# Attention block and MLP on one core: projection weights read in place, in pairs, instead of through a permuted copy

## The chip, the cores and the metric

The kernel runs on one core of a Trainium2 chip. The metric is the device time in microseconds of one execution. Profiled times come from one further execution, recorded by the hardware profiler: its span runs from the first to the last instruction, and its own time is somewhat longer than the span.

## The reference

One sequence of 2048 rows, 576 columns, bf16. `A_*` and `B_*` are the inputs.

```python
def _A_ref(x, wqkv, wo):          # x: layer norm of the input
    H = 32; Dh = 18; W, dil = 8, 2
    qkv = (x @ wqkv).reshape(B, S, 3, H, Dh).transpose(2, 0, 3, 1, 4)
    q, k, v = qkv[0], qkv[1], qkv[2]
    idx = pos[:, None] - arange(W)[None, :] * dil      # 8 keys: the row itself, 2 back, 4 back ...
    kg, vg = k, v gathered at idx                      # (B, H, S, W, Dh)
    logits = einsum("bhsd,bhswd->bhsw", q, kg) * Dh ** -0.5   # idx < 0 masked with -1e9
    attn = softmax(logits)
    o = einsum("bhsw,bhswd->bhsd", attn, vg)
    return o.transpose(0, 2, 1, 3).reshape(B, S, D) @ wo

def _B_ref(x, w1, b1, w2, b2):    # hidden width 4608
    return gelu(layernorm(x) @ w1 + b1) @ w2 + b2

h = x + _A_ref(layernorm(x), wqkv, wo)
out = h + _B_ref(h, w1, b1, w2, b2)
```

A column of the Q, K or V part of `wqkv` is numbered by head and dimension: column `h * 18 + d`.

## The kernel before

The 2048 rows are dealt to 16 tiles of 128 rows so that row `16 p + j` lies in partition `p` of tile `j`. The key that lies two rows back is then in the same partition, in the tile two before, and the eight keys of a row are eight tiles of one parity. `kwin[e]` and `vwin[e]` hold the eight K and V tiles of parity `e`. When tile `n` has been used, its K and V slots are replaced by the same tile shifted by one partition, through DRAM (`kvd`, written by `bounce`, read back into the slots by the loads `ks` and `vs`, lines 520 and 522). Row 0 of `kvd` is zero.

The work is written as named tasks with an engine, a cost, a priority and the tasks that must come first. `Weaver.run` is a planner: it takes, again and again, the ready task that could start first by the costs, and issues its instructions. Each engine then runs its instructions in that order; the costs decide the order and nothing else. Buffers are counted as slots in the planner (`pm`, three PSUM tiles; `lg`, `prod`, `q` and so on).

The tasks of a tile `n`:

- `ln1a`, `ln1r`, `ln1b`: layer norm. VectorE takes the statistics (line 314), their aggregate (315) and the variance with the epsilon (`ln_var`, 318), GpSimd raises it to the power -1/2 (322), VectorE (tiles 0 to 7) or ScalarE (357, tiles 8 to 15, with `nmr` from GpSimd, 349) normalizes in place.
- `t1`, `t1e`: the transposition, for tiles 0 to 7 by TensorE (329) and a copy by ScalarE (373), for the others by a DMA. The transposed tiles 0 to 6 lie for a while in the space of `vwin[1]`, those of later tiles in `kwin[1]`, which gives the names in the profile.
- `cK`, `cV`, `cQ`: the projections (394), a chunk each of two halves of 288 columns times five blocks of 128 rows of the contraction, so ten matmuls with a moving operand `wqkv_sb` of 128 x 288. `eK`, `eV`, `eQ`: eviction to bf16 by ScalarE (406).
- `p1a` to `p1b`, `ex`, `p2n`, `p2a`, `p2s`, `p2b`: the attention, on VectorE but for the exponential (ScalarE, 468). K times q for eight slots at once (445, 4608 elements); a tree of additions over the 18 dimensions (451) and the last addition into `lg` (458); maximum over the slots (438 to 440), difference (464); after the exponential the sum over the slots (again 438 to 440), its reciprocal (476) and `at = lg * rden` (479); V times `at` (486) and a tree over the slots (492 to 498).
- `t2`, `wo`, `woe`, `ln2a`, `hb`, `ln2m`, `ln2b`, `t3`: output projection (564), residual (577), second layer norm and its transposition.

Two tiles form a group `g` of the MLP: nine units `u` (630: first matrix; 641: gelu on ScalarE), then the second matrix in four passes (667), and the addition of `hb` on VectorE (686) and the store.

The tree of line 451 needs all heads of one dimension side by side, that is columns numbered `d * 32 + h`. The kernel gets this order by permuting the weights: the Q, K and V parts of `wqkv` are loaded into `wraw`, and 15 copies, `perm{t}{kt}` (line 290, six on ScalarE, nine on VectorE), write them to `wqkv_sb` in the other order, reading every 18th element. The K copies come first; those of V and Q are put on ScalarE and VectorE between the tasks of tiles 2 to 8. `wo` is loaded with its rows in the same order (`wo_load`, 212). `wraw` and `zrow`, the zero row for `kvd`, lie in a pool that is closed before the first part of `w2` is loaded, into the same space (`w2_chunk`, 236); that load waits for all permutations.

SP issues nearly all DMAs in the planned order: x tiles, V and Q weights, biases, `wo`, `w1` (18 parts, 223), the transposes (371, 541), the bounces (426, 427), `w2` (18 parts). ScalarE's queue issues the K weights.

Of the kernel before, what the change touches and what calls it, by code (L numbers as in the profile page):

```python
# [90 lines left out]
def kernel(  # L91
# [48 lines left out]
    wo_sb = wpool.tile([P, KC, HALF], BF16, name="wo_sb")  # L140
    hn_bufs = [wpool.tile([P, KC, 2 * P], BF16, name="hnT0")]
    b1_raw = wpool.tile([FT, P], BF16, name="b1_raw")
# [13 lines left out]
    raw_cm = tc.tile_pool(name="raw", bufs=1, side="right")  # L156
    raw = raw_cm.__enter__()
    wraw = raw.tile([P, 3, KT, D], BF16, name="wraw")
    zrow = raw.tile([NT, 2 * D], BF16, name="zrow")

    late, w2p = {}, {}
# [35 lines left out]
    def wq_load(eng, t, k0, k1):  # L197
        def fn():
            src = bass.AP(tensor=A_wqkv.tensor, offset=A_wqkv[k0 * P, t * D].offset,
                          ap=[[3 * D, P], [P * 3 * D, k1 - k0], [1, D]])  # L200
            eng.dma_start(out=wraw[:, t, k0:k1, :], in_=src)
        return fn

    def wq_rest(eng, t):
        return lambda: eng.dma_start(out=wraw[0:64, t, 4, :], in_=A_wqkv[512:576, t * D:(t + 1) * D])

    def wo_load(half, dd):
        def fn():
            src = bass.AP(tensor=A_wo.tensor, offset=A_wo[dd, half * HALF].offset,
                          ap=[[Dh * D, H], [2 * D, KC], [1, HALF]])  # L210
            p0 = 64 * half + 32 * dd
            nc.sync.dma_start(out=wo_sb[p0:p0 + 32, :, :], in_=src)
        return fn
# [12 lines left out]
    def b1_load():  # L226
        nc.sync.dma_start(out=b1_raw[:], in_=B_b1.rearrange("(f p) -> f p", p=P))

    def w2_chunk(c):
        def fn():  # L230
            if "w2" not in w2p:
                raw_cm.__exit__(None, None, None)
                pool = ctx.enter_context(tc.tile_pool(name="w2p", bufs=1, side="right"))
                w2p["w2"] = pool.tile([P, FT, D], BF16, name="w2_sb")
            f0, f1 = c * FT // W2C, (c + 1) * FT // W2C
            nc.sync.dma_start(out=w2p["w2"][:, f0:f1, :],
                              in_=B_w2[f0 * P:f1 * P, :].rearrange("(ft p) c -> p ft c", p=P))
        return fn
# [16 lines left out]
    def b2_load():  # L255
        nc.sync.dma_start(out=b2_bc[:], in_=B_b2.partition_broadcast(P))
        nc.sync.dma_start(out=kvd[:, 0, :], in_=zrow[:])
# [3 lines left out]
    wos = [f"WO{half}{dd}" for half in range(2) for dd in range(2)]  # L261
    for half in range(2):
        for dd in range(2):
            bulk(f"WO{half}{dd}", wo_load(half, dd), 166, prio=10)
# [5 lines left out]
    perms = [f"perm{t}{kt}" for t in range(3) for kt in range(KT)]  # L270
    for c in range(W2C):
        bulk(f"w2{c}", w2_chunk(c), 295, prio=30 + c, after=perms + ["b2"])
# [7 lines left out]
    nc.gpsimd.memset(zrow[:], 0.0)  # L280
# [3 lines left out]
    for t in range(3):  # L284
        for kt in range(KT):
            def perm(t=t, kt=kt, on=None):
                rows = P if kt < KT - 1 else D - kt * P
                src = wraw[0:rows, t, kt, :].rearrange("p (h d) -> p d h", h=H, d=Dh)
                dst = wqkv_sb[0:rows, kt, t * D:(t + 1) * D].rearrange("p (d h) -> p d h", d=Dh, h=H)
                {"ACT": nc.scalar.copy, "DVE": nc.vector.tensor_copy}[on](out=dst, in_=src)  # L290
            on = "ACT" if kt in (1, 3) else "DVE"
            add(f"perm{t}{kt}", on, {"ACT": 1.23, "DVE": 0.65}[on], lambda f=perm, on=on: f(on=on),
                (f"W{t}{'aabbc'[kt]}",) + ((("ln1b0",) if kt == 2 else ()) if t == K else (f"t1e{2 + 2 * t}" if on == "ACT" else f"ln1b{W - 1}",)),
                prio=(-18, -100, -17)[t])
# [43 lines left out]
    def front(n):  # L338
# [36 lines left out]
        add(f"ln1a{n}", "DVE", 1.2, ln1a, (f"x{n}",) + (("ln1b0",) if n == 1 else ()), prio=-20 + n if n < W else 0.5 + (n - W) // 4)  # L375
        add(f"ln1r{n}", "POOL", 0.6 if n < W else 1.1, ln1r, (f"ln1a{n}",), prio=-20, lag=0.1 if n < W else 1.0)
# [10 lines left out]
        def chunk(t):  # L387
            def fn():
                pq = ps_pm.tile([P, 2, 512], F32, tag="pm", name="pq")
                T["pq", n, t] = pq  # L390
                for half in range(2):
                    c0 = t * D + half * HALF
                    for kt in range(KT):
                        nc.tensor.matmul(pq[:, half, 0:HALF], lhsT=T["xnT", n][:, kt, :],  # L394
                                         rhs=wqkv_sb[:, kt, c0:c0 + HALF],
                                         start=(kt == 0), stop=(kt == KT - 1))
            return fn

        def evict(t):
            def fn():  # L400
                if t == Q:
                    T["q", n] = wpool.tile([P, D], BF16, tag="q", name="q", bufs=NQ)
                    dst = T["q", n][:]
                else:
                    dst = (kwin if t == K else vwin)[e][:, s, :]
                nc.scalar.copy(out=dst.rearrange("p (a c) -> p a c", a=2), in_=T["pq", n, t][:, :, 0:HALF])  # L406
            return fn
# [23 lines left out]
    def attention(n):  # L431
# [16 lines left out]
        def p1b(steps):  # L448
            pv = T["prod", n][:].rearrange("p w (d h) -> p w d h", d=Dh, h=H)
            for a, b in steps:  # L450
                nc.vector.tensor_tensor(out=pv[:, :, 0:b - a, :], in0=pv[:, :, 0:b - a, :],  # L451
                                        in1=pv[:, :, a:b, :], op=ALU.add)
# [17 lines left out]
        def p2n():  # L470
# [6 lines left out]
            at = sb.tile([P, W, H], BF16, tag="at", name="at", bufs=1)  # L477
            T["at", n] = at
            nc.vector.tensor_tensor(out=at[:], in0=lg[:], in1=rden[:].unsqueeze(1).to_broadcast([P, W, H]),
                                    op=ALU.mult)  # L480

        def p2a():
# [22 lines left out]
        add(f"p1s{n}", "DVE", 1.37, lambda: p1b(((9, 18),)), (f"p1a{n}",), prio=n)  # L505
        add(f"p1t{n}", "DVE", 1.5, lambda: p1b(((4, 8), (2, 4), (1, 2))), (f"p1s{n}",), prio=n)
# [6 lines left out]
        add(f"p2n{n}", "DVE", 1.35, p2n, [f"ex{n}"] + ([f"p2a{n - 1}"] if n else []), prio=-8 + n, give=(f"lg{n}",))  # L513
# [103 lines left out]
    def mlp(g):  # L617
# [115 lines left out]
```

## Time and profile before

| | |
|---|---|
| median of 3 runs | 390.32 us (389.94 to 390.32) |
| the profiled execution | 389.9 us, of it span 388.1 us |
| TensorE's granted clock over the span | 1.000 |
| TensorE, matmuls | 373.1 us busy, 4607 instructions |
| VectorE | 297.1 us, 559 |
| ScalarE | 220.5 us, 447 |
| GpSimd | 37.2 us, 65 |
| projections (394), matmuls | 480, in 210 + 210 + 60 by the tile that holds the transposed rows |
| share of the 16 DMA engines, 6.7 to 26.5 us | 1.0 |

Times are in microseconds from the start of the span unless marked ns. PE is TensorE, PEld its weight loads, DVE VectorE, ACT ScalarE, POOL GpSimd, SP the engine that issues DMAs. A group line names the source line, engine, operation, output from input, shapes and count; then busy time and the mean duration of one in ns; then the idle time of the engine just before and what ended it. Matmuls are pipelined: the mean duration of one is longer than its share of a row of them, which the timeline shows. A line of the waits reads: who waited, for whom, us in total, how often, the longest.

### The profile page before, as it was taken

What the parts mean: (1) busy time and instruction counts of PE and PEld (TensorE: products, weight loads), DVE (VectorE), ACT (ScalarE), POOL (GpSimd) and SP (SyncE); (2) the same over time, 40 slices, a digit from 0 to 9 for tenths busy, and PEclk for the clock granted to TensorE, in tenths of its full rate; (3) what the DMA queues carried; (4) which work ended last, traced back from release to release, by engine and by line L of the source; (5) the groups of instructions that cost most, each with busy time, mean ns of one, the idle gap of its engine ahead of it and who ended that gap; (6) DMA issues with size and microseconds to landing.
All of it is one profiled execution on the core that took longest, in us unless ns stands there. A gap on an engine that the chain in (4) does not pass through costs nothing.

```text
span 388.1 us, 10761 instructions
## 1 busy us (share of the span) xinstructions
PE 373.1 (96%) x4607; PEld 305.2 (79%) x4607; DVE 297.1 (77%) x559; ACT 220.5 (57%) x447; POOL 37.2 (10%) x65
## 2 busy tenths in 40 slices
PE   2889999999899999999999999999999999999996
PEld 1667877788777887887788878887888788778875
DVE  5999999999999999999999998989976952000000
ACT  4697767688914974188227823790487068306700
POOL 6455010101001000001100010110011011000000
PEclk9999999999999999999999999999999999999999
DMA  8988899887232402127333214222312432100000
GB/s 264 277 165 227 213 212 272 254 255 235 57 83 51 105 19 61 33 63 63 70 77 73 61 48 94 63 47 76 78 37 43 108 64 21 29 15 19 2 15 17
DMA packets 63968, 38.48 MB, mean 99 GB/s; under 512 B 39520, under 2 KB 63904, under 8 KB 63920
## 3 DMA queue, kind: packets, MB, share of 16 engines
q1 hardware_dynamic: 63296, 37.13, 40.4%
q8 instruction: 36, 0.59, 0.7%
q10 hardware_dynamic: 624, 0.66, 0.5%
q14 instruction: 12, 0.10, 0.1%
HBM read 22.28 MB, written 6.52 MB: 74 GB/s over the span
## 4 chain that ended last, share of the span: by engine, by line
PE 74%; DVE 12%; issue 1%; ACT 1%; DVEq 0%; ACTq 0%
PE po L667 37%; PE pm L630 33%; PE pw L564 4%; DVE prod L445 3%; DVE prod L451 2%; DVE prod L486 1%; ACT hT L641 1%; DVE prod L492 1%; DVE l_st L314 1%; DVE h L577 1%; DVE hb L590 1%; DVE half L438 0%; DVE prod L496 0%; DVE half L439 0%; DVE lg L458 0%
## 5 line engine op out<-in xcount | busy, mean ns | idle before, releaser
L641 ACT ACTIVATE hT<-pm,b_sb 128x256 bf16<-128x256 f32 x288 | 111.9, 482 | 82.1 <-PE pm L630 81.8
L630 PE MATMUL pm<-hnT,w_sb 64*128 64x256 bf16 x2592 | 144.5, 269 | 0.8 <-ACT hT L641 0.8
L667 PE MATMUL po<-w_sb,hT 128*128 128x288 bf16 x1152 | 143.2, 286 | 0.0
L630 PEld LDWEIGHTS <-w_sb 64*128 64x128 bf16 x2592 | 125.9, 94 | 17.7 <-issue 2.4
L667 PEld LDWEIGHTS <-hT 128*128 128x128 bf16 x1152 | 111.7, 98 | 30.6 <-issue 2.4
L686 DVE TENSOR_TENSOR osb<-po,hb 128x288 bf16<-128x288 f32 x32 | 14.4, 453 | 57.1 <-PE po L667 57.1
L322 POOL TENSOR_TENSOR l_rs<-l_ve,mhalf 128x1 f32<-128x1 f32 x32 | 28.4, 888 | 287.8 <-DVE l_ve L318 287.8
L451 DVE TENSOR_TENSOR prod<-prod 128x2304 bf16<-128x2304 bf16 (+1 forms) x64 | 44.2, 690 | 1.8
L486 DVE TENSOR_TENSOR prod<-vwin,at 128x4608 bf16<-128x4608 bf16 x16 | 40.9, 2554 | 0.4
L445 DVE TENSOR_TENSOR prod<-kwin,q 128x4608 bf16<-128x4608 bf16 x16 | 40.9, 2555 | 0.3
L394 PE MATMUL pq<-wqkv_sb,vwin 128*128 128x288 bf16 x210 | 30.1, 303 | 3.2 <-ACT vwin L373 1.8
L594 ACT ACTIVATE hn<-h,nmr,l_rs 128x576 bf16<-128x576 f32 (+1 forms) x32 | 19.2, 651 | 23.0 <-issue 11.6
L394 PEld LDWEIGHTS <-vwin 128*128 128x128 bf16 x210 | 21.2, 103 | 10.5 <-ACT vwin L373 2.6
L394 PE MATMUL pq<-wqkv_sb,kwin 128*128 128x288 bf16 x210 | 27.2, 286 | 0.0
L394 PEld LDWEIGHTS <-kwin 128*128 128x128 bf16 x210 | 20.3, 98 | 5.4 <-issue 0.5
L492 DVE TENSOR_TENSOR prod<-prod 128x2304 bf16<-128x2304 bf16 x16 | 21.7, 1358 | 0.6
L569 ACT COPY h<-pw 128x576 f32<-128x576 f32 x16 | 10.4, 651 | 19.4 <-PE pw L564 19.4
L564 PE MATMUL pw<-wo_sb,oT 64*128 64x288 bf16 x288 | 20.3, 283 | 0.0
L577 DVE TENSOR_TENSOR h<-h,xr 128x576 f32<-128x576 f32 x16 | 12.0, 752 | 9.6 <-ACT h L569 9.6
L564 PEld LDWEIGHTS <-oT 64*128 64x128 bf16 x288 | 13.5, 94 | 4.5 <-issue 1.4
L406 ACT CAST kwin<-pq 128x576 bf16<-128x576 f32 x16 | 10.2, 648 | 8.5 <-PE pq L394 8.3
L314 DVE BATCH_NORM_STATS2 l_st<-h 128x6 f32<-128x288 f32 x32 | 13.1, 452 | 0.6
(62 smaller groups left out, 238.2 us busy)
## 6 DMA issues: line engine op xcount, KB each, us to landing
w_sb<-in_B_w_dram SPq DMA_DIRECT2D x36, 288.0 KB, 4.7
xr<-in_A_x_dram SPq DMA_DIRECT2D x16, 144.0 KB, 2.3
out_dram<-osb SPq DMA_DIRECT2D x16, 144.0 KB, 1.8
kvd<-kwin SPq DMA_DIRECT2D x14, 144.0 KB, 4.1
kvd<-vwin SPq DMA_DIRECT2D x14, 144.0 KB, 3.7
kwin<-kvd SPq DMA_DIRECT2D x14, 144.0 KB, 2.5
vwin<-kvd SPq DMA_DIRECT2D x14, 144.0 KB, 2.1
wraw<-in_A_wqkv_dram SPq DMA_DIRECT2D x4, 288.0 KB, 4.1
```

The costliest lines, as they stand in the source:

```text
L314: nc.vector.bn_stats(out=st[:, c, :], in_=src[:, c * HALF:(c + 1) * HALF])
L322: nc.gpsimd.tensor_tensor(out=L["rs"][:, n, :], in0=L["ve"][:, n, :], in1=mhalf[:], op=ALU.pow)
L394: nc.tensor.matmul(pq[:, half, 0:HALF], lhsT=T["xnT", n][:, kt, :], rhs=wqkv_sb[:, kt, c0:c0 + HALF], start=(kt == 0), stop=(kt == KT - 1))
L445: nc.vector.tensor_tensor(out=prod[:], in0=kwin[e][:], in1=T["q", n][:].unsqueeze(1).to_broadcast([P, W, D]), op=ALU.mult)
L451: nc.vector.tensor_tensor(out=pv[:, :, 0:b - a, :], in0=pv[:, :, 0:b - a, :], in1=pv[:, :, a:b, :], op=ALU.add)
L486: nc.vector.tensor_tensor(out=prod[:].rearrange("p w (d h) -> p w d h", d=Dh, h=H), in0=vwin[e][:].rearrange("p w (d h) -> p w d h", d=Dh, ...
L492: nc.vector.tensor_tensor(out=prod[:, 0:4, :], in0=prod[:, 0:4, :], in1=prod[:, 4:8, :], op=ALU.add)
L564: nc.tensor.matmul(pw[:, half, 0:HALF], lhsT=T["oT", n][lo:lo + 64, block(c, half), :], rhs=wo_sb[lo:lo + 64, c, :], start=(c == 0), stop= ...
L594: nc.scalar.activation(out=hn_slots[n % 2][:, c0:c1], in_=src, func=ACT.Identity, scale=L2["rs"][:, n, :], bias=nmr[:, n, :])
L630: nc.tensor.matmul(pm[:, half, q, 0:width], lhsT=w1_sb[lo:lo + 64, c, f0:f0 + P], rhs=T["hnT", g][lo:lo + 64, block(c, half), 0:width], st ...
L641: nc.scalar.activation(out=T["hT", g, u][:, half, q, 0:width], in_=T["pm", g, u][:, half, q, 0:width], func=ACT.Gelu_apprx_tanh, bias=b1_s ...
L667: nc.tensor.matmul(T["po", n, half][:], lhsT=T["hT", g, u][:, r, q, a * P:(a + 1) * P], rhs=w2p["w2"][:, ft, half * HALF:(half + 1) * HALF ...
```

## The change

The permutation is gone. The weights are loaded into `wqkv_sb` as they are, and the matmul's moving operand is a strided view of them: for a half, nine pairs of dimensions `k`, 16 heads `h` and the two dimensions `r` of a pair, two adjacent elements and then a step of 18 elements (36 bytes). The projection comes out as `k, h, r` within a half, and the eviction puts the two halves together to `k, (h, r)`, rows of 64. The tree over the dimensions becomes one over the nine pairs, the last addition is over `r`, and `at` is written twice, for both `r`, so that V times `at` has rows of 64. `wo`'s rows are loaded to match, to every second partition.

With it, `w2_sb` gets space of its own from the start; `b1_raw` and the zero row lie in it until its parts are loaded. For tiles 0 to 7 `ln_var` goes from VectorE to GpSimd. Four costs in the planner are changed (`ln1a`, `ln1r`, `p2n`, and the `perm` tasks are gone), so the planner's order moves in places: of the first tiles, the second and third transposes of TensorE follow each other, and the first Q chunk comes before the eighth K chunk; in SP's queue some `w1` parts come later, and eight instead of five parts of `w2` follow a K reload.

```diff
+    w2_sb = wpool.tile([P, FT, D], BF16, name="w2_sb")
+    b1_raw = w2_sb[0:FT, 2, 0:P]
...
-    wraw = raw.tile([P, 3, KT, D], BF16, name="wraw")
-    zrow = raw.tile([NT, 2 * D], BF16, name="zrow")
...
-            eng.dma_start(out=wraw[:, t, k0:k1, :], in_=src)
+            eng.dma_start(out=wqkv_sb[:, k0:k1, t * D:(t + 1) * D], in_=src)
...
-            p0 = 64 * half + 32 * dd
-            nc.sync.dma_start(out=wo_sb[p0:p0 + 32, :, :], in_=src)
+            nc.sync.dma_start(out=wo_sb[64 * half + r:64 * half + 64:2, :, :], in_=src)
...
-        nc.sync.dma_start(out=kvd[:, 0, :], in_=zrow[:])
+        nc.sync.dma_start(out=kvd[:, 0, :], in_=w2_sb[0:NT, 0:2, :].rearrange("p a c -> p (a c)"))
...
-        bulk(f"w2{c}", w2_chunk(c), 295, prio=30 + c, after=perms + ["b2"])
+        bulk(f"w2{c}", w2_chunk(c), 295, prio=30 + c, after=("b2", "b1t"))
...
-    for t in range(3):
-        for kt in range(KT):
-            def perm(t=t, kt=kt, on=None):
-                rows = P if kt < KT - 1 else D - kt * P
-                src = wraw[0:rows, t, kt, :].rearrange("p (h d) -> p d h", h=H, d=Dh)
-                dst = wqkv_sb[0:rows, kt, t * D:(t + 1) * D].rearrange("p (d h) -> p d h", d=Dh, h=H)
-                {"ACT": nc.scalar.copy, "DVE": nc.vector.tensor_copy}[on](out=dst, in_=src)
...
         def ln1a():
             ln_stats(L1, n, T["x", n][:, 0:D])
-            ln_var(nc.vector, L1, n, (1.0, EPS))
+            if n >= W:
+                ln_var(nc.vector, L1, n, (1.0, EPS))
 
         def ln1r():
+            if n < W:
+                ln_var(nc.gpsimd, L1, n, (1.0, EPS))
             ln_rstd(L1, n)
...
-                    c0 = t * D + half * HALF
                     for kt in range(KT):
+                        cols = wqkv_sb[:, kt, t * D:(t + 1) * D].rearrange("p (h k r) -> p k h r", h=H, r=2)
                         nc.tensor.matmul(pq[:, half, 0:HALF], lhsT=T["xnT", n][:, kt, :],
-                                         rhs=wqkv_sb[:, kt, c0:c0 + HALF],
+                                         rhs=cols[:, :, half * H // 2:(half + 1) * H // 2, :],
                                          start=(kt == 0), stop=(kt == KT - 1))
...
-                nc.scalar.copy(out=dst.rearrange("p (a c) -> p a c", a=2), in_=T["pq", n, t][:, :, 0:HALF])
+                nc.scalar.copy(out=dst.rearrange("p (k a c) -> p a k c", a=2, c=H),
+                               in_=T["pq", n, t][:, :, 0:HALF].rearrange("p a (k c) -> p a k c", c=H))
...
-            pv = T["prod", n][:].rearrange("p w (d h) -> p w d h", d=Dh, h=H)
+            pv = T["prod", n][:].rearrange("p w (k c) -> p w k c", c=2 * H)
...
-            nc.vector.tensor_tensor(out=lg[:], in0=pv[:, :, 0, :], in1=pv[:, :, 8, :], op=ALU.add)
+            nc.vector.tensor_tensor(out=lg[:], in0=pv[:, :, :, 0], in1=pv[:, :, :, 1], op=ALU.add)
...
-            at = sb.tile([P, W, H], BF16, tag="at", name="at", bufs=1)
+            at = sb.tile([P, W, H, 2], BF16, tag="at", name="at", bufs=1)
...
-            nc.vector.tensor_tensor(out=at[:], in0=lg[:], in1=rden[:].unsqueeze(1).to_broadcast([P, W, H]),
-                                    op=ALU.mult)
+            nc.vector.tensor_tensor(out=at[:], in0=lg[:].unsqueeze(3).to_broadcast([P, W, H, 2]),
+                                    in1=rden[:].unsqueeze(1).unsqueeze(3).to_broadcast([P, W, H, 2]), op=ALU.mult)
...
-                                    in1=at[:].unsqueeze(2).to_broadcast([P, W, Dh, H]), op=ALU.mult)
+            pairs = at[:].rearrange("p w h r -> p w (h r)")
+                                    in1=pairs.unsqueeze(2).to_broadcast([P, W, Dh // 2, 2 * H]), op=ALU.mult)
...
-        add(f"p1s{n}", "DVE", 1.37, lambda: p1b(((9, 18),)), (f"p1a{n}",), prio=n)
-        add(f"p1t{n}", "DVE", 1.5, lambda: p1b(((4, 8), (2, 4), (1, 2))), (f"p1s{n}",), prio=n)
+        add(f"p1s{n}", "DVE", 1.37, lambda: p1b(((5, 9),)), (f"p1a{n}",), prio=n)
+        add(f"p1t{n}", "DVE", 1.5, lambda: p1b(((3, 5), (2, 3), (1, 2))), (f"p1s{n}",), prio=n)
```

More of the change, by code (lines that the diff above doesn't have):

```diff
@@ L140 @@
     wo_sb = wpool.tile([P, KC, HALF], BF16, name="wo_sb")
+    w2_sb = wpool.tile([P, FT, D], BF16, name="w2_sb")
+    b1_raw = w2_sb[0:FT, 2, 0:P]
     hn_bufs = [wpool.tile([P, KC, 2 * P], BF16, name="hnT0")]
-    b1_raw = wpool.tile([FT, P], BF16, name="b1_raw")
     b1_sb = wpool.tile([P, FT], F32, name="b1_sb")
@@ L155 @@
     wqkv_sb = early.tile([P, KT, 3 * D], BF16, name="wqkv_sb")
-    raw_cm = tc.tile_pool(name="raw", bufs=1, side="right")
-    raw = raw_cm.__enter__()
-    wraw = raw.tile([P, 3, KT, D], BF16, name="wraw")
-    zrow = raw.tile([NT, 2 * D], BF16, name="zrow")
-    late, w2p = {}, {}
+    late = {}
     def late_pool():
@@ L200, in fn, with wo_load @@
                           ap=[[3 * D, P], [P * 3 * D, k1 - k0], [1, D]])
-            eng.dma_start(out=wraw[:, t, k0:k1, :], in_=src)
+            eng.dma_start(out=wqkv_sb[:, k0:k1, t * D:(t + 1) * D], in_=src)
         return fn
     def wq_rest(eng, t):
-        return lambda: eng.dma_start(out=wraw[0:64, t, 4, :], in_=A_wqkv[512:576, t * D:(t + 1) * D])
-    def wo_load(half, dd):
+        return lambda: eng.dma_start(out=wqkv_sb[0:64, 4, t * D:(t + 1) * D], in_=A_wqkv[512:576, t * D:(t + 1) * D])
+    def wo_load(half, r):
         def fn():
-            src = bass.AP(tensor=A_wo.tensor, offset=A_wo[dd, half * HALF].offset,
+            src = bass.AP(tensor=A_wo.tensor, offset=A_wo[r, half * HALF].offset,
                           ap=[[Dh * D, H], [2 * D, KC], [1, HALF]])
-            p0 = 64 * half + 32 * dd
-            nc.sync.dma_start(out=wo_sb[p0:p0 + 32, :, :], in_=src)
+            nc.sync.dma_start(out=wo_sb[64 * half + r:64 * half + 64:2, :, :], in_=src)
         return fn
@@ L226, in b1_load @@
     def b1_load():
-        nc.sync.dma_start(out=b1_raw[:], in_=B_b1.rearrange("(f p) -> f p", p=P))
+        nc.sync.dma_start(out=b1_raw, in_=B_b1.rearrange("(f p) -> f p", p=P))
     def w2_chunk(c):
         def fn():
[L231 to L234, printed above, removed]
             f0, f1 = c * FT // W2C, (c + 1) * FT // W2C
-            nc.sync.dma_start(out=w2p["w2"][:, f0:f1, :],
+            nc.sync.dma_start(out=w2_sb[:, f0:f1, :],
                               in_=B_w2[f0 * P:f1 * P, :].rearrange("(ft p) c -> p ft c", p=P))
@@ L256, in b2_load @@
         nc.sync.dma_start(out=b2_bc[:], in_=B_b2.partition_broadcast(P))
-        nc.sync.dma_start(out=kvd[:, 0, :], in_=zrow[:])
+        nc.sync.dma_start(out=kvd[:, 0, :], in_=w2_sb[0:NT, 0:2, :].rearrange("p a c -> p (a c)"))
     load("b2", b2_load, 150, prio=8.5, issue=0.7, transfers=2)
     load("b1", b1_load, 20, prio=9.0)
-    wos = [f"WO{half}{dd}" for half in range(2) for dd in range(2)]
+    wos = [f"WO{half}{r}" for half in range(2) for r in range(2)]
     for half in range(2):
-        for dd in range(2):
-            bulk(f"WO{half}{dd}", wo_load(half, dd), 166, prio=10)
+        for r in range(2):
+            bulk(f"WO{half}{r}", wo_load(half, r), 166, prio=10)
     w1s = [[f"w1{c}{half}{k}" for half in range(2) for k in range(0, KC, W1K)] for c in range(W1C)]
@@ L269 @@
                 bulk(f"w1{c}{half}{k}", w1_chunk(c, half, k), 295, prio=20 + c)
-    perms = [f"perm{t}{kt}" for t in range(3) for kt in range(KT)]
     for c in range(W2C):
-        bulk(f"w2{c}", w2_chunk(c), 295, prio=30 + c, after=perms + ["b2"])
+        bulk(f"w2{c}", w2_chunk(c), 295, prio=30 + c, after=("b2", "b1t"))
     nc.gpsimd.memset(mhalf[:], -0.5)
@@ L279 @@
     nc.gpsimd.memset(wqkv_sb[64:128, KT - 1, :], 0.0)
-    nc.gpsimd.memset(zrow[:], 0.0)
+    nc.gpsimd.memset(w2_sb[0:NT, 0:2, :], 0.0)
     for n in range(1, NT):
         nc.gpsimd.memset(T["x", n][:, D:DP], 0.0)
-    for t in range(3):
-        for kt in range(KT):
-            def perm(t=t, kt=kt, on=None):
-                rows = P if kt < KT - 1 else D - kt * P
-                src = wraw[0:rows, t, kt, :].rearrange("p (h d) -> p d h", h=H, d=Dh)
-                dst = wqkv_sb[0:rows, kt, t * D:(t + 1) * D].rearrange("p (d h) -> p d h", d=Dh, h=H)
[L290 to L294, printed above, removed]
     def b1_turn():
         T["b1T"] = ps_pm.tile([P, 2048], BF16, tag="pm", name="b1T")[:, 0:FT]
-        nc.tensor.transpose(T["b1T"], b1_raw[:], ident[0:FT, 0:FT])
+        nc.tensor.transpose(T["b1T"], b1_raw, ident[0:FT, 0:FT])
     add("b1t", "PE", 0.1, b1_turn, ("b1",), prio=-35, take=("pm", "b1t"), lag=0.3)
@@ L373, in t1e @@
                 nc.scalar.copy(out=T["xnT", n], in_=T["pt1", n])
-        add(f"ln1a{n}", "DVE", 1.2, ln1a, (f"x{n}",) + (("ln1b0",) if n == 1 else ()), prio=-20 + n if n < W else 0.5 + (n - W) // 4)
-        add(f"ln1r{n}", "POOL", 0.6 if n < W else 1.1, ln1r, (f"ln1a{n}",), prio=-20, lag=0.1 if n < W else 1.0)
+        add(f"ln1a{n}", "DVE", 1.07 if n < W else 1.2, ln1a, (f"x{n}",) + (("ln1b0",) if n == 1 else ()), prio=-20 + n if n < W else 0.5 + (n - W) // 4)
+        add(f"ln1r{n}", "POOL", 0.95 if n < W else 1.1, ln1r, (f"ln1a{n}",), prio=-20, lag=0.1 if n < W else 1.0)
         add(f"ln1b{n}", "DVE" if n < W else "ACT", 0.45 if n < W else 0.7, ln1b, (f"ln1r{n}",), prio=-20 + n)
@@ L412, in front @@
             first = t == K and n < W
-            add(f"c{n}{'QKV'[t]}", "PE", 1.24, chunk(t), [f"t1e{n}"] + [f"perm{t}{kt}" for kt in range(KT)],
+            add(f"c{n}{'QKV'[t]}", "PE", 1.24, chunk(t), [f"t1e{n}"] + [f"W{t}{part}" for part in "abc"],
                 prio=-50 + n if first else -25 if n == 0 and t == Q else -24 + n if t == V and n < W else -10 + n + 0.2 * r,
@@ L454, in p1c @@
         def p1c():
-            pv = T["prod", n][:].rearrange("p w (d h) -> p w d h", d=Dh, h=H)
+            pv = T["prod", n][:, :, 0:2 * H].rearrange("p w (h r) -> p w h r", r=2)
             lg = sb.tile([P, W, H], F32, tag="lg", name="lg", bufs=LG)
             T["lg", n] = lg
-            nc.vector.tensor_tensor(out=lg[:], in0=pv[:, :, 0, :], in1=pv[:, :, 8, :], op=ALU.add)
+            nc.vector.tensor_tensor(out=lg[:], in0=pv[:, :, :, 0], in1=pv[:, :, :, 1], op=ALU.add)
             if s + 1 < W:
@@ L485, in p2a @@
             T["prod2", n] = prod
-            nc.vector.tensor_tensor(out=prod[:].rearrange("p w (d h) -> p w d h", d=Dh, h=H),
-                                    in0=vwin[e][:].rearrange("p w (d h) -> p w d h", d=Dh, h=H),
-                                    in1=at[:].unsqueeze(2).to_broadcast([P, W, Dh, H]), op=ALU.mult)
+            pairs = at[:].rearrange("p w h r -> p w (h r)")
+            nc.vector.tensor_tensor(out=prod[:].rearrange("p w (k c) -> p w k c", c=2 * H),
+                                    in0=vwin[e][:].rearrange("p w (k c) -> p w k c", c=2 * H),
+                                    in1=pairs.unsqueeze(2).to_broadcast([P, W, Dh // 2, 2 * H]), op=ALU.mult)
         def p2s():
@@ L512, in attention @@
         ready = [f"e{m}V" for m in same] + [f"vs{m}" for m in before]
-        add(f"p2n{n}", "DVE", 1.35, p2n, [f"ex{n}"] + ([f"p2a{n - 1}"] if n else []), prio=-8 + n, give=(f"lg{n}",))
+        add(f"p2n{n}", "DVE", 1.6, p2n, [f"ex{n}"] + ([f"p2a{n - 1}"] if n else []), prio=-8 + n, give=(f"lg{n}",))
         add(f"p2a{n}", "DVE", 2.57, p2a, ready + [f"p2n{n}"] + ([f"p2b{n - 1}"] if n else []), prio=-8 + n,
@@ L667, in fn @@
                             nc.tensor.matmul(T["po", n, half][:], lhsT=T["hT", g, u][:, r, q, a * P:(a + 1) * P],
-                                             rhs=w2p["w2"][:, ft, half * HALF:(half + 1) * HALF],
+                                             rhs=w2_sb[:, ft, half * HALF:(half + 1) * HALF],
                                              start=(u + q + r == 0), stop=(u == UN - 1 and q + r == 2))
```

## Prediction

> **What bounds the kernel now.** The page comes first. Its two lines on engines and on the chain of waits say that TensorE works for 373.1 of the 388.1 us, and that the chain that ended last is TensorE's for three quarters.
>
> ```profile
> PE 373.1 (96%) x4607; PEld 305.2 (79%) x4607; DVE 297.1 (77%) x559; ACT 220.5 (57%) x447; POOL 37.2 (10%) x65
> ...
> PE 74%; DVE 12%; issue 1%; ACT 1%; DVEq 0%; ACTq 0%
> ```
>
> The list of PE's waits shows the 15.0 us in which it does not work: 6.7 us before the first transpose, 5.1 us in eight waits, and some 3 us behind the last matmul (the last addition on VectorE and the store).
>
> ```profile
> PE pt L329 <- DVE kwin L354: 6.7, 1, 6.7
> PE pq L394 <- ACT vwin L373: 1.8, 3, 0.8
> PE pq L394 <- ACT kwin L373: 1.0, 1, 1.0
> PE pm L630 <- ACT hT L641: 0.8, 1, 0.8
> PE pt L329 <- ACT hT L641: 0.8, 1, 0.8
> PE pt L329 <- ACT q L406: 0.4, 1, 0.4
> PE pq L394 <- ACT vwin L406: 0.3, 1, 0.3
> ```
>
> So whatever is taken from ScalarE and VectorE can shorten the run only through these waits, and whatever is added to a matmul is paid in full. The timeline of the first 30 us is the next view (start, duration, engine, line, operation). The first Q/K/V chunk starts at 8.21 us and takes 2.58 us, a chunk in full flow 1.27 us (60 matmuls in 7.61 us, 127 ns each). VectorE starts the attention at 28.92 us, when the eighth K chunk and the first Q chunk are evicted and the layer-norm work queued ahead is done.
>
> ```profile
> 8.21 2.58 PE L394 MATMUL pq<-wqkv_sb,vwin 128*128 128x288 bf16 x10 [0.79 <-ACT vwin L373]
> ...
> 12.12 2.58 PE L394 MATMUL pq<-wqkv_sb,vwin 128*128 128x288 bf16 x10 [0.79 <-ACT vwin L373]
> ...
> 24.14 1.39 PE L394 MATMUL pq<-wqkv_sb,vwin 128*128 128x288 bf16 x10 [0.95 <-ACT kwin L373]
> ...
> 25.37 1.39 PE L394 MATMUL pq<-wqkv_sb,kwin 128*128 128x288 bf16 x10
> ...
> 26.59 7.61 PE L394 MATMUL pq<-wqkv_sb,vwin 128*128 128x288 bf16 x60
> ...
> 28.92 2.56 DVE L445 TENSOR_TENSOR prod<-kwin,q 128x4608 bf16<-128x4608 bf16 x1
> ```
>
> Last, the groups by form give the prices of what is removed and changed (busy us, mean ns of one).
>
> ```profile
> L290 ACT COPY wqkv_sb<-wraw 128x576 bf16<-128x576 bf16 x6 | 7.5, 1243 | 0.8 <-DMA wraw<-in_A_wqkv_dram 0.8
> ...
> L290 DVE COPY wqkv_sb<-wraw 128x576 bf16<-128x576 bf16 x6 | 3.9, 675 | 0.0
> ...
> L290 DVE COPY wqkv_sb<-wraw 64x576 bf16<-64x576 bf16 x3 | 2.0, 666 | 0.0
> ...
> L406 ACT CAST q<-pq 128x576 bf16<-128x576 f32 x16 | 10.2, 639 | 5.1 <-PE pq L394 5.0
> ...
> L451 DVE TENSOR_TENSOR prod<-prod 128x2304 bf16<-128x2304 bf16 x16 | 21.7, 1356 | 0.4
> ...
> L479 DVE TENSOR_TENSOR at<-lg,rden 128x256 bf16<-128x256 f32 x16 | 6.8, 425 | 0.6
> ...
> L440 DVE TENSOR_TENSOR den<-half 128x32 f32<-128x32 f32 x16 | 3.1, 192 | 0.6
> ```
>
> **The change, part by part.**
>
> Permutations removed: 7.5 us of ScalarE, 3.9 + 2.0 = 5.9 us of VectorE, all before 26 us.
>
> Variance step of the first eight tiles moved from VectorE (154 ns each, 1.2 us) to GpSimd. GpSimd's queue holds memsets until 5.68 us, so the first one runs there at 5.68 instead of on VectorE at 4.69. GpSimd's small tensor_scalar (the nmr step alone) takes 0.27 us: the first transpose comes about 0.3 us later, near 7.0. For later tiles GpSimd needs about 0.27 + 0.67 us, under VectorE's 1.43 us per tile (0.81 + 0.21 + 0.42, without the variance; 1.50 us from tile to tile now).
>
> The layer-norm line on VectorE: first normalization done near 7.0, then eight statistics (about 1.0 us with gaps; the order puts tile 8's among them) and seven normalizations of 0.43: 7.0 + 8.0 + 3.0 = 18.0 us for tile 7, against 19.6 now. Six more statistics at 1.16 us: 25.0 us. VectorE stops being what the attention waits for at 28.92.
>
> But TensorE is then its own bound in the head. It runs in order, and the new order puts the first Q chunk ahead of the eighth K chunk. Worked forward: transposes 7.0, first chunk 8.5 to 11.1 (2.58, the slow form), two transposes to 12.4, eviction of the second to 12.65. Behind it: a second chunk at 2.58 or less, a third at 1.6, transposes of 0.45 to 0.5 and five chunks at 1.27. At the slow price for the second chunk this puts the eighth K chunk at 12.65 + 2.58 + 0.5 + 1.6 + 3 x 1.72 + 2 x 1.27 + 0.45 = 25.5 us; at the fast price, 24.2. Now it starts at 25.37 with the Q chunk still behind it, 1.27 us of work. The gain of TensorE is so 1.1 to 2.4 us. The slow form goes with little work before it: the third chunk, with steadier work from 14.5 us on, takes 1.68 us, the fourth 1.39. With fewer pauses it should end somewhat sooner, so I take 2.3 us, near the upper end.
>
> Attention: the eighth K eviction is then at about 26.6 us, 2.3 us earlier, and one statistics step fewer stands behind it (1.16 us). The normalized weights (at, L479) are written twice: 512 elements for 256. From 32 to 256 elements of f32 the rows go 192 to 425 ns, 1.04 ns each, so 425 + 256 x 1.04 = 691 ns, 0.27 us more per tile. Four tiles lie on VectorE's part of the chain (45 to 95 us): 1.1 us given back. VectorE's gain at 95 us is 2.3 + 1.16 - 1.1 = 2.4 us, level with TensorE's, so the two waits for ScalarE's gelu (0.8 us each) stay. After 99 us TensorE runs without a stop; the other twelve tiles' 3.2 us lie on a VectorE that has 57.1 us of waiting on L686 alone. Cover gone, they would cost 3.2 us.
>
> Costs at nothing: the tree over pairs adds 2048, 1024, 512, 512 elements for 2304, 1024, 512, 256; at 0.52 ns per element (1356 and 687 ns for 2304 and 1024) that is -133 and +133 ns. The broadcast of p2a keeps an unbroken inner run (64 for 32) and its 2.55 us. The eviction writes runs of 32, 64 bytes; I leave it at 0.64 us, and ScalarE has 10.2 us of copies in the 12 us from 8 to 20 after losing the permutations; slower by half it would hold TensorE there. SP's queue keeps its transfers; six w1 issues fall behind transposes, but the first matmul that needs them is near 80 us. The last w2 chunk is issued at 93 us now and lands near 97, needed at 103; in the new order eight chunks stand behind a kwin reload instead of five, about 2 us more against some 6 of margin.
>
> Strided moving operand: the one open price, and the one that decides. 480 matmuls read 144 pairs of 4 bytes, 36 bytes apart, where they read 288 adjacent elements. No row shows TensorE reading so. Lower end: 0 ns, the stream hides it. The two permutation copies read with the same 36-byte step, one element per step. ScalarE: 1243 - 639 (the eviction of as many elements) = 604 ns over 576 steps, 1.05 ns per step; 144 steps would add 151 ns. VectorE: at most 675 / 576 = 1.17 ns per step; 144 steps take 169 ns, 42 more than 127. TensorE halved (258 ns, the row at 8.21): 131 more. Ends so: 0 and 480 x 151 ns = 72 us. [...] 4.8 ns per matmul (2.3 us / 480) already eats the gain.
>
> [...]
>
> Sum: 388.1 - 2.3 = 385.8 us of span, 387.6 with the 1.8 us around it (389.9 in the profiled execution). The median of the runs stands 0.4 above that execution: 388.0. What the measurement can tell from no change is about 0.2%, 0.8 us.
>
> **The rivals.**
> 1. TensorE at half rate in the 480 matmuls. Place: from 16 us to where the projections end, now 82 us, TensorE nearly full. Price 131 ns x 450 (the first 30 are slow already) = 59 us, to 63 for all 480: 388 + 59 to 63 = 447 to 451; by ScalarE's price up to 460. For it: ScalarE's copy, with the same step, takes twice its eviction. Against: two elements per step, not one. It decides from 4.8 ns per matmul on. Chance 0.27.
> 2. A partial loss, by VectorE's bound 42 ns: 388 + 20 = 408; from 5 to 80 ns, 390 to 426. Chance 0.13.
> 3. The reads are free but the head gives nothing: the slow form lasts as long in time, GpSimd's longer step delays each tile, or 2 to 6 ns per matmul eat it. 389.5 to 391. Chance 0.10.
> That the permutations are not gone can't be: no copy to the weights is left in any engine's order.
>
> **How the numbers follow.** The forecast, free reads, has 0.50, its own range 386 to 389.6 (gain 0.7 to 4.3 us, the end where all of the five microseconds of waits but a little goes). Faster: 0.45 of it and 0.02 of rival 3, 0.47. Same: 0.03 and 0.04, 0.07. Slower: 0.02, 0.04, 0.13 and 0.27, 0.46. With both signs so near, the range must reach into rival 1: 386 to 452; outside lie ScalarE's price and a larger gain.
>
> **What would show it.** Right: the pq group at 286 to 303 ns mean and 60 matmuls in about 7.6 us; the eighth K chunk near 24.5 and the first attention product near 26.6 us; at at 0.69 us; the second and third chunk sooner at full rate; PE busy near 373 us. Wrong: chunks of ten at 1.7 us (rival 2) or 2.5 us (rival 1) with PE's busy time up by 20 or 60 us, and L406 waiting for pq for most of 16 to 140 us; for rival 3, the first product later than 28 us with pq unchanged.

## The result, and the profile after

The changed kernel takes 449.96 us (median of 4 runs, 449.57 to 450.32), the kernel before 390.19 us beside it: ratio 1.1533, 95% interval 1.1513 to 1.1552. It is 60 us slower. The forecast, 388.0 us, is far off; the time lies inside the wide range only because rival 1 (TensorE at half rate in the 480 projection matmuls, 447 to 451 us) was in it, and that rival is what happened.

The two lines of the page again, engines and then the chain that ended last:

```profile
PE 435.1 (97%) x4607; PEld 312.8 (70%) x4607; DVE 295.8 (66%) x542; ACT 215.2 (48%) x441; POOL 33.3 (7%) x73
...
PE 93%; ACT 3%; DMA 3%; SPq 0%; issue 0%; DVE 0%
```

TensorE works 62 us more (373.1 before) with the same 4607 matmuls, and its share of the span is still nearly all. VectorE and ScalarE have lost a little work, as meant, and VectorE, with 12% of the chain before, has left it. The list of PE's waits:

```profile
PE pt L309 <- DVE kwin L337: 6.7, 1, 6.7
PE pq L377 <- DMA wqkv_sb<-in_A_wqkv_dram: 2.3, 4, 1.3
PE pq L377 <- ACT vwin L356: 0.3, 1, 0.3
PE pm L615 <- ACT hT L626: 0.2, 1, 0.2
```

No wait grew that would explain 60 us; the sum behind the first transpose fell from 5.1 to 2.8 us. New is that the first chunks wait for the weights' own transfer, where the copies used to wait for it (2.3 us now, 0.8 before). So the time is inside the matmuls. The timeline of the chunks (start, duration, engine, line, operation), and the VectorE row with the first attention product:

```profile
20.24 2.74 PE L377 MATMUL pq<-wqkv_sb,vwin 128*128 128x288 bf16 x10
...
36.77 18.26 PE L377 MATMUL pq<-wqkv_sb,vwin 128*128 128x288 bf16 x70
54.85 2.76 PE L377 MATMUL pq<-wqkv_sb,kwin 128*128 128x288 bf16 x10
57.43 15.68 PE L377 MATMUL pq<-wqkv_sb,vwin 128*128 128x288 bf16 x60
...
81.30 1.28 PE L549 MATMUL pw<-wo_sb,oT 64*128 64x288 bf16 x18
...
37.65 2.56 DVE L429 TENSOR_TENSOR prod<-kwin,q 128x4608 bf16<-128x4608 bf16 x1 [12.88 <-ACT kwin L389]
```

Sixty matmuls take 15.68 us where they took 7.61. From the start of the row of 70 to the start of the next row (36.77 to 54.85 us) it is 18.08 us, 258 ns each, against 127. The output projection between them (L549) keeps its 1.28 us. VectorE's first product now comes 8.7 us later than before, after 12.9 us of waiting for the K evictions. The groups that were to change on VectorE and ScalarE (busy us, mean ns of one) did as expected:

```profile
L389 ACT CAST q<-pq 128x576 bf16<-128x576 f32 x16 | 10.2, 639 | 26.7 <-PE pq L377 26.7
...
L435 DVE TENSOR_TENSOR prod<-prod 128x2048 bf16<-128x2048 bf16 x16 | 19.6, 1222 | 0.3
...
L463 DVE TENSOR_TENSOR at<-lg,rden 128x512 bf16<-128x512 f32 x16 | 11.1, 692 | 0.6
```

### The profile page after: what moved, and what is told of

The parts are those of the page before. It is cut to its first block, busy times and chain, and to the rows that moved or that the text cites. A ratio compares the mean times of both kernels' runs of the same rounds, so it can differ in the third digit from the quotient of the medians.

```text
span 447.7 us, 10750 instructions
## 1 busy us (share of the span) xinstructions
PE 435.1 (97%) x4607; PEld 312.8 (70%) x4607; DVE 295.8 (66%) x542; ACT 215.2 (48%) x441; POOL 33.3 (7%) x73
## 4 chain that ended last, share of the span: by engine, by line
PE 93%; ACT 3%; DMA 3%; SPq 0%; issue 0%; DVE 0%
PE po L652 32%; PE pm L615 29%; PE pq L377 27%; PE pw L549 4%; DMA wqkv_sb<-in_A_wqkv_dram 3%; ACT hT L626 2%; PE pt L309 1%; ACT L626 0%; ACT L452 0%; ACT hn L579 0%; ACT h L554 0%; DVE osb L671 0%; SPq L198 0%; ACT lg L452 0%; SPq L191 0%
## 5 line engine op out<-in xcount | busy, mean ns | idle before, releaser
L377 PE MATMUL pq<-wqkv_sb,vwin 128*128 128x288 bf16 x210 | 56.2, 437 | 2.6 <-DMA wqkv_sb<-in_A_wqkv_dram 2.3
L377 PE MATMUL pq<-wqkv_sb,kwin 128*128 128x288 bf16 x210 | 55.8, 437 | 0.0
L429 DVE TENSOR_TENSOR prod<-kwin,q 128x4608 bf16<-128x4608 bf16 x16 | 40.9, 2556 | 20.7 <-ACT kwin L389 12.9
L302 POOL TENSOR_TENSOR l_rs<-l_ve,mhalf 128x1 f32<-128x1 f32 x32 | 24.8, 774 | 347.3 <-DVE l_ve L298 346.7
L377 PEld LDWEIGHTS <-vwin 128*128 128x128 bf16 x210 | 24.0, 116 | 31.3 <-ACT vwin L356 2.1
L435 DVE TENSOR_TENSOR prod<-prod 128x2048 bf16<-128x2048 bf16 (+1 forms) x64 | 44.2, 690 | 1.7
L377 PEld LDWEIGHTS <-kwin 128*128 128x128 bf16 x210 | 23.8, 115 | 28.6 <-issue 0.5
L389 ACT CAST kwin<-pq 128x576 bf16<-128x576 f32 x16 | 10.2, 639 | 29.8 <-PE pq L377 29.8
L389 ACT CAST vwin<-pq 128x576 bf16<-128x576 f32 x16 | 10.2, 639 | 27.3 <-PE pq L377 27.3
L389 ACT CAST q<-pq 128x576 bf16<-128x576 f32 x16 | 10.2, 639 | 26.7 <-PE pq L377 26.7
L549 PE MATMUL pw<-wo_sb,oT 64*128 64x288 bf16 x288 | 20.3, 283 | 0.0
```

Source lines behind the costliest of these rows:

```text
L302: nc.gpsimd.tensor_tensor(out=L["rs"][:, n, :], in0=L["ve"][:, n, :], in1=mhalf[:], op=ALU.pow)
L389: nc.scalar.copy(out=dst.rearrange("p (k a c) -> p a k c", a=2, c=H), in_=T["pq", n, t][:, :, 0:HALF].rearrange("p a (k c) -> p a k c", c=H))
L429: nc.vector.tensor_tensor(out=prod[:], in0=kwin[e][:], in1=T["q", n][:].unsqueeze(1).to_broadcast([P, W, D]), op=ALU.mult)
L549: nc.tensor.matmul(pw[:, half, 0:HALF], lhsT=T["oT", n][lo:lo + 64, block(c, half), :], rhs=wo_sb[lo:lo + 64, c, :], start=(c == 0), stop= ...
```

## The experiments

**Undo the strided read alone (e1_adjacent).**

```diff
-                                         rhs=cols[:, :, half * H // 2:(half + 1) * H // 2, :],
+                                         rhs=wqkv_sb[:, kt, c0:c0 + HALF],
```

> The changed kernel with the moving operand of the 480 projection matmuls taken as 288 adjacent columns again; all else as changed. Its columns come out in another order than the attention takes them, so the output is not the reference's. Theory (the whole loss lies in the strided reads of TensorE): chunks of ten back at 1.27 us, PE busy near 373 us, and the time falls to the forecast's sum for free reads, 388.0 us (386 to 389.6), below the kernel before. Rival (the attention over pairs, GpSimd's longer step or the new order of the queues also cost): clearly above 390, by up to some 10 us.

Measured: 386.39 us, ratio to before 0.9901 (0.9885 to 0.9918). The rows of PE:

```profile
23.36 1.40 PE L377 MATMUL pq<-wqkv_sb,kwin 128*128 128x288 bf16 x10
24.59 8.97 PE L377 MATMUL pq<-wqkv_sb,vwin 128*128 128x288 bf16 x70
```

and VectorE's first product:

```profile
25.76 2.56 DVE L429 TENSOR_TENSOR prod<-kwin,q 128x4608 bf16<-128x4608 bf16 x1 [1.94 <-ACT kwin L389]
```

The 70 matmuls take 8.97 us for 18.26. Everything else in the change together gains 3.6 us on the kernel before; the strided read alone costs 449.96 - 386.39 = 63.6 us, of which PE's busy time holds 63.0 (435.1 against 372.1).

**Do the strided read alone (e2_before_pairs).** The kernel before, with the one line turned the other way.

> The kernel before, permuting copies and attention unchanged, with only the moving operand read as pairs 36 bytes apart; the output is not the reference's. Theory (the loss lies in the strided reads alone): 258 ns per matmul in place of 127, 450 to 480 times 131 ns, 59 to 63 us more: 449 to 453 us. Rival (the loss needs the rest of the change): near 390 us.

Measured: 449.32 us, ratio 1.152 (1.1503 to 1.1537), PE busy 434.8 us. With the permuting copies and the attention over dimensions in place the loss is the same, so no other part of the change is needed for it. The gains and losses do not add: from before, 390, to e1, 386.4, is a gain of 3.6, but with the slow reads in both kernels it is nil (449.3 against 450.0). The profiles show where it goes: with slow reads PE works 435 us and waits 2.8 us behind its first transpose in both kernels; with adjacent reads it works 373.1 us and waits 5.1 in the kernel before, and 372.1 and 3.1 in e1.

**What in the pattern costs (e3_runs).** The same step of 36 bytes, other lengths of a run: K single elements, V runs of 3, Q runs of 6.

```diff
+   K: rhs = mine.rearrange("p (h k r) -> p k h r", h=H, r=1)[:, :, hs, :]
+   V: rhs = mine.rearrange("p (h k r) -> p k h r", h=H, r=3)[:, :, hs, :]
+   Q: rhs = mine.rearrange("p (h k r) -> p k h r", h=H, r=6)[:, :, hs, :]
```

> The changed kernel, its moving operand read in runs of another length with the same step of 36 bytes between heads: K single elements, V runs of 3, Q runs of 6 (output not the reference's). Theory A (a fixed time for every 16-byte line that the stream comes to, 258 / 144 = 1.79 ns, hidden below 127 ns): lines per matmul 288, 120, 72, so 516, 215 and 129 ns for K, V and Q; time 388 + 160 x (0.389 + 0.088 + 0.002) = 465 us. Theory B (any operand that is not one adjacent run goes at half rate): 258 ns for all three, 451 us. Theory C (a fixed price per jump, 131 / 144 = 0.91 ns, added to 127): 288, 96 and 48 jumps, 389, 214 and 171 ns, 451 us.

Measured: 473.33 us in one run. K is line L381 here, V L383, Q L385:

```profile
20.48 5.31 PE L381 MATMUL pq<-wqkv_sb,vwin 128*128 128x288 bf16 x10
25.61 0.71 PE L309 MATMUL pt<-ident,kwin 128*128 128x128 bf16 x5
...
71.51 2.33 PE L383 MATMUL pq<-wqkv_sb,kwin 128*128 128x288 bf16 x10
73.68 8.81 PE L385 MATMUL pq<-wqkv_sb,vwin 128*128 128x288 bf16 x60
82.33 1.60 PE L385 MATMUL pq<-wqkv_sb,kwin 128*128 128x288 bf16 x10
```

From start to start of the next row: K (20.48 to 25.61) 513 ns, V (71.51 to 73.68) 217, Q (73.68 to 82.33) 144. Theory B, the same half rate for whatever is not adjacent, is out, and so is theory C, which wanted 389 for K. Theory A, a time per 16-byte line, has K and V; its 129 for Q is too low for the 144 measured. Put as "a line costs at least the time of four columns, and with more than four the time of these", a column at the 0.44 ns of adjacent reads (127 / 288), it gives 148 for Q, and this form was tested next. The run's time is 8 us above theory A's 465 us; stretches with a lower granted clock go with that (last section).

**Lines against adjacency (e4_steps and e5_lines).** Patterns that part the line from the run: pairs in steps of 8 and of 16 bytes, every second and every fourth element, runs of 4 in steps of 16 bytes, runs of 9.

```diff
+   e4: K row.rearrange("p (g s) -> p g s", s=4)[:, :, 0:2]   V s=2, [0:1]   Q runs of 9, step 36 bytes
+   e5: K row.rearrange("p (g s) -> p g s", s=8)[:, :, 0:2]   V s=8, [0:4]   Q s=4, [0:1]
```

> The changed kernel with other moving operands (output not the reference's): K pairs in steps of 8 bytes (half of every 16-byte line), V every second element, Q runs of 9 with the step of 36 bytes. [...] K and V take four columns from each of 72 lines: 127 ns as for adjacent reads; Q 336 cycles, 140 ns and the few ns that adjacent reads show above 120, so 147; time 386.4 + 160 x 0.020 = 390 us. Theory B (half rate unless adjacent): 258 ns for all, 449 us. Theory D (the unit is 8 bytes, 1.79 ns each): 144, 144 and 96 units, 258, 258 and 172 ns, 435 us.

Measured: 392.16 us in one run, 2 us above the sum of 390 us; PE waits 2.5 us in it for the transfer of the weights, which it does not in e1. No run shows the 140 ns for 336 columns, or the 120 for 288, from which Q's 147 was put together: adjacent reads took 127 ns for 288 columns, which makes 148 for 336, and Q took 144. K, V and Q are lines L381, L383, L385:

```profile
27.75 9.12 PE L383 MATMUL pq<-wqkv_sb,vwin 128*128 128x288 bf16 x70
36.70 1.44 PE L383 MATMUL pq<-wqkv_sb,kwin 128*128 128x288 bf16 x10
37.98 8.80 PE L385 MATMUL pq<-wqkv_sb,vwin 128*128 128x288 bf16 x60
46.62 1.60 PE L385 MATMUL pq<-wqkv_sb,kwin 128*128 128x288 bf16 x10
...
48.57 1.44 PE L381 MATMUL pq<-wqkv_sb,kwin 128*128 128x288 bf16 x10
49.84 1.44 PE L383 MATMUL pq<-wqkv_sb,kwin 128*128 128x288 bf16 x10
```

> The changed kernel with other moving operands (output not the reference's): K pairs in steps of 16 bytes (two columns from every line), V runs of 4 in steps of 16 bytes (four from every line), Q every fourth element (two from every line, not adjacent). Theory A (4 cycles per line at least): 258, 127 and 258 ns; time 386.4 + 160 x 0.262 = 428 us. Theory B (half rate unless adjacent): 258 for all, 449 us. Theory D (8-byte units): 144, 72 and 288 units, 258, 129 and 516 ns, 470 us. Theory C (0.91 ns per jump): 144, 72 and 288 jumps, 258, 193 and 389 ns, 460 us.

Measured: 426.57 us in one run, near theory A's 428; the other theories wanted 449 to 470.

```profile
35.24 9.14 PE L383 MATMUL pq<-wqkv_sb,vwin 128*128 128x288 bf16 x70
44.22 1.44 PE L383 MATMUL pq<-wqkv_sb,kwin 128*128 128x288 bf16 x10
45.50 15.52 PE L385 MATMUL pq<-wqkv_sb,vwin 128*128 128x288 bf16 x60
60.84 2.74 PE L385 MATMUL pq<-wqkv_sb,kwin 128*128 128x288 bf16 x10
...
71.61 2.74 PE L381 MATMUL pq<-wqkv_sb,kwin 128*128 128x288 bf16 x10
74.17 1.46 PE L383 MATMUL pq<-wqkv_sb,kwin 128*128 128x288 bf16 x10
```

All patterns, each from the start of its row to the start of the next one (a line is counted as 16 bytes, eight columns):

| moving operand, 288 columns | lines | jumps | ns per matmul |
|---|---|---|---|
| adjacent | 36 | 0 | 127 |
| runs of 4, step 16 bytes (e5 V) | 72 | 72 | 128 |
| pairs, step 8 bytes (e4 K) | 72 | 144 | 127 |
| every second element (e4 V) | 72 | 288 | 128 |
| runs of 9, step 36 bytes (e4 Q) | 64 | 32 | 144 |
| runs of 6, step 36 bytes (e3 Q) | 72 | 48 | 144 |
| runs of 3, step 36 bytes (e3 V) | 120 | 96 | 217 |
| every fourth element (e5 Q) | 144 | 288 | 256 |
| pairs, step 16 bytes (e5 K) | 144 | 144 | 256 |
| pairs, step 36 bytes (the change) | 144 | 144 | 258 |
| single elements, step 36 bytes (e3 K) | 288 | 288 | 513 |

What counts in these patterns is how many columns each line gives, not the jumps or adjacency: every second element, with 288 jumps, is free (128 ns), and pairs are free or cost double (127 or 256) by how many of them lie in one line. A line from which only one or two columns are taken costs 256 / 144 = 1.78 ns (513 / 288 too), four columns' time at the full rate (4 x 0.44); three are not enough either (217 / 120 = 1.81 ns in e3 V, where most lines give three). A line that gives more than four is taken to cost their time, eight columns 3.5 ns as in the adjacent reads (127 / 36): runs of 9 are so not free although they touch only 64 lines, since some of these give eight columns and some one. This makes 336 columns' time of runs of 9 and of 6, 148 ns, a little more than the 144 measured. Theory D, 8-byte units, wanted 258 for e4's K and V and 516 for e5's Q, which took 127, 128 and 256; it is out. So are units of 32 bytes: pairs in steps of 16 bytes would give four columns to each and be free, and took 256.

**The order made by the eviction (e6_evict_order).** The weights unpermuted, the matmul reading adjacent columns, ScalarE reordering while it evicts, attention over dimensions as before.

```diff
+   K, Q: copy(out=dst.rearrange("p (d a h) -> p a d h", ...), in_=pq.rearrange("p a (h d) -> p a d h", ...))  # steps in the read
+   V:    copy(out=dst.rearrange("p (d a h) -> p a h d", ...), in_=pq.rearrange("p a (h d) -> p a h d", ...))  # steps in the write
```

> A version without permutation of weights and with adjacent reads: the weights stay as they are, the matmul reads 288 adjacent columns, and ScalarE puts the columns in order (dimension, head) while it evicts the projection; attention as before. For K and Q it reads PSUM in steps of 18 f32 and writes runs of 16, for V it reads adjacent and writes every 32nd bf16 element. Theory 1 (steps cost ScalarE what they cost in the permuting copies, 1.05 ns per element): 1.24 us per eviction in place of 0.64, 48 x 0.6 = 29 us more of ScalarE before the projections end, of which ScalarE's idle time there covers most; 390 to 405 us. Theory 2 (PSUM reads or bf16 writes in steps are free): 0.64 us on that side, and the time falls with e1, 386 to 389 us.

Measured: 407.73 us, ratio 1.0455 (1.0432 to 1.0478). The groups of the evictions, V is L390:

```profile
L390 ACT CAST vwin<-pq 128x576 bf16<-128x576 f32 x16 | 42.8, 2727 | 3.1 <-PE pq L377 3.0
...
L393 ACT CAST q<-pq 128x576 bf16<-128x576 f32 x16 | 11.4, 719 | 1.7 <-PE pq L377 1.6
L393 ACT CAST kwin<-pq 128x576 bf16<-128x576 f32 x16 | 10.6, 663 | 5.8 <-PE pq L377 5.8
```

The time is above the range of either theory. Both were wrong for V: single bf16 written 64 bytes apart cost 2.73 us, more than twice what theory 1 gave. Reading PSUM in steps is nearly free (663 and 719 ns against 639). PE waits 11.5 us for the V evictions in this run.

**Stepped reads for all three (e8_evict_read).** As e6, with the K and Q form for V too.

> A version meant to beat both kernels: weights unpermuted, matmuls read 288 adjacent columns, and ScalarE's eviction reads PSUM in steps of 18 f32 (663 to 719 ns in the mixed version) and writes runs of 16 bf16 in the order (dimension, head); attention as in the kernel before, so the normalized weights are written once (0.42 us). Against the version with adjacent reads, 386.4 us: 4 x 0.27 = 1.1 us less on VectorE's part of the chain, and 0.02 to 0.08 us more for each of 48 evictions, 16 of them before the attention starts. 385 to 387 us if stepped PSUM reads cost no more than that; above 390 if they slow down when all three are read so.

Measured: 387.34 us (387.32 to 387.70), ratio 0.9937 (0.9925 to 0.9948); evictions 637 to 642 ns. VectorE is relieved by 4.6 us against e1 (its groups add up to 302.0 us for 306.6), yet it is not faster than e1, and a little above the 385 to 387 us expected: PE now waits 3.1 us for gelu (1.7 in e1). That a relief of VectorE goes into ScalarE's gelu at the start of the MLP is read from these waits, not tested.

**The variance step back on VectorE (e7_var_vector).** e1 with `ln_var` of tiles 0 to 7 on VectorE.

> The version with adjacent reads and one more part undone: the variance step of tiles 0 to 7 back on VectorE, with its old planner costs (output not the reference's, as in that version). Theory (the gain of 3.6 us comes from the missing permutations and the order of the chunks; where the variance step runs is worth little, since TensorE is the bound of the head): 386.4, within 0.5 us. Rival (VectorE's 1.2 us are part of the gain): 387.3 to 387.9 us.

Measured: 386.63 us median, but six runs between 386.6 and 389.16, ratio 0.9941 (0.9918 to 0.9963). The interval overlaps e1's. The median goes with the theory; a microsecond either way can't be told.

**A version that beats both (e9_evict_pairs).** The change with adjacent reads and the order over pairs made in the eviction.

```diff
+   copy(out=dst.rearrange("p (k a h r) -> p a k h r", ...), in_=pq.rearrange("p a (h k r) -> p a k h r", ...))
```

> The changed kernel with adjacent reads on TensorE, and the order over pairs made by the eviction instead: ScalarE reads PSUM in pairs of f32 in steps of 18 and writes runs of 32; attention over pairs as changed. It computes the reference. If reading PSUM so costs ScalarE nothing, as in steps of single f32 (638 to 642 ns), it takes the time of the version with adjacent reads, 386.4 us (385.9 to 387.3). If a pattern of one more dimension slows ScalarE, 48 evictions take longer than 0.70 us and the time is above 388.

Measured: 385.97 us (385.81 to 387.02), ratio 0.9897 (0.9880 to 0.9913). The groups:

```profile
L389 ACT CAST vwin<-pq 128x576 bf16<-128x576 f32 x16 | 10.3, 644 | 5.2 <-PE pq L377 5.1
L389 ACT CAST kwin<-pq 128x576 bf16<-128x576 f32 x16 | 10.2, 638 | 8.6 <-PE pq L377 8.5
L389 ACT CAST q<-pq 128x576 bf16<-128x576 f32 x16 | 10.2, 635 | 5.4 <-PE pq L377 5.3
```

The evictions take what they took before (639 to 648 ns), so the reordering is free here. The time is 3.9 us, 1%, below the kernel before beside it (389.88 us): the gain of e1 is had, in an order that the attention can use.

## Why the prediction was wrong, step by step

**The strided moving operand: the step that failed.** The bounds were 0 and 151 ns per matmul, and the forecast stands on 0, the author's estimate, which no run shows; 131 was measured. Two elements per step, not one, was the point held against rival 1; e5 shows that two from a line still take twice the time (256 ns), and e4 that four are enough (127 ns). VectorE's permuting copy could not settle it: a row of 1.17 ns per step cannot show a loss of the size that matters on TensorE, where a column takes 0.44 ns. Of the two copies ScalarE's was the nearer row: 604 ns over 576 steps, 1.05 ns each, against 131 / 144 = 0.91 ns. A comparison of these rows would have warned: the two columns of a pair take 0.88 ns on TensorE (2 x 0.44), and neither copy shows a step that short (2.16 and 1.17 ns, the element's own time included).

**Rival 1** had its place and its time right: 447 to 451, measured 449.96. Its discount for the first 30 matmuls fits e2, whose loss of 59.4 us is 453 times 131 ns. But the row it was priced from, 258 ns in the first chunk, has another cause: that chunk takes 2.58 us in e1 with adjacent reads as well. And from start to start of the next row (8.21 to 10.59 us in the kernel before) it is 238 ns per matmul, not 258. So the exact price was luck.

**The rest of the sum** can be judged in e1, where the slow read is away: 2.3 us forecast, 3.6 measured. The first transpose came at 6.74 us, not 7.0: the last six memsets ahead of it on GpSimd took 0.14 us each instead of 0.27 (in the kernel before a copy of VectorE, 0.68 us from 4.76 us on, lies beside them; whether it is why was not tested), and GpSimd's first variance step took 0.19, not 0.27. The eighth K chunk started at 23.36, forecast near 24.5, since only the first two chunks were slow (2.58 and 2.41 us) and the third took 1.39, not 1.6. VectorE's first product came at 25.76 us, forecast 26.6. The two waits for gelu stayed (0.9 and 0.8 us), as forecast. The price of `at` (691 forecast, 692 measured), the tree at nothing and the eviction at 0.64 us held, and no wait for `w2` appeared. ScalarE had less to do than the text counted: by TensorE's rows in e1 five evictions of 0.64 us and six copies of 0.70 lie between 8 and 20 us, 7.4 us as an estimate, not 10.2. The DMA wait of the first chunks, 2.3 us in the changed kernel, was not foreseen. It is in the profiles of e4 (2.5) and e5 (1.4) too and not in those of e1 and e3, whose instructions stand in the same order; why is open.

**The chances.** 0.50 stood on free reads, with bounds of 0 and 72 us that no row narrowed, and 0.40 on rivals 1 and 2; ScalarE's row deserved the larger share.

## What to carry to other kernels

On a kernel bound by TensorE, price a strided moving operand as the eleven patterns here came out (127 to 513 ns for 288 columns of bf16): count the columns taken from each 16-byte line, and below four add what is missing at 0.44 ns per column (measured at a granted clock of 1.00), times every matmul. If an order has to be changed, look for the engine that reads PSUM anyway: an eviction by ScalarE that reads PSUM in steps and writes runs cost the same as one that doesn't (635 to 644 ns in e8 and e9, 663 and 719 beside slow ones in e6, against 639), while one that writes single bf16 elements 64 bytes apart cost 2.73 us. Before betting on an access pattern, put several patterns in one kernel on lines of their own; three runs settled here what no row of the first profile showed.

## What the runs showed of the hardware, unexpected

In e3, where K's matmuls take 513 ns, the granted clock fell at times (0.942 over the span), and matmuls that read adjacent columns slowed with it. The view by stretches of time (length, then busy us of PE, PEld, DVE, ACT, POOL, then the granted clock, the share of the DMA engines and GB/s):

```profile
71.50:84.00 12.50, 12.50 (x86) 7.99 (x85) 10.07 (x10) 5.91 (x10) 0.00 (x0) 1.00 0.57 143
84.00:92.00 8.00, 8.00 (x30) 2.67 (x29) 3.03 (x9) 2.27 (x3) 0.00 (x0) 0.71 0.63 153
92.00:104.00 12.00, 12.00 (x52) 5.01 (x52) 8.73 (x15) 3.51 (x6) 0.99 (x1) 0.78 0.36 89
```

PE counts as busy throughout. The 0.71 and 0.78 are means of their stretches. The output projection that starts at 91.90 us, 18 matmuls, takes 2.34 us, for 1.26 at 168.55 us, where the clock is 1.00. K's own chunks do not change:

```profile
37.41 5.32 PE L381 MATMUL pq<-wqkv_sb,vwin 128*128 128x288 bf16 x10
...
50.84 5.29 PE L381 MATMUL pq<-wqkv_sb,kwin 128*128 128x288 bf16 x10
```

The first lies in a stretch with a mean clock of 1.00 (8 to 42.5 us), the second in one of 0.77 (42.5 to 56). The pairs of the changed kernel show the same: the chunk at 17.36 us, with a clock of 0.50 from 17 to 19 us, takes 2.76 us, and the one at 20.24, at 1.00, 2.74. So in these rows the price of a line is a time, some 1.78 ns, that did not grow when the clock was halved: "four columns" holds at 1.00.

The changed kernel has one such stretch, 0.57 on the mean between 16 and 20 us; e2's clock is 0.996 over the span as well. Why the clock fell was not shown; e5, with 256 ns per matmul for K and Q, shows 1.000 over its span.
